# Rewriting the order of all steps in a fused GateLoop and SoLU kernel

## The chip, the cores and the metric

The kernel runs on one core of one Trainium2 chip. The metric is the device time of one execution in microseconds (us). A time quoted for a kernel is the median of its executions; stretches, waits and idle times are those of its one profiled execution. Every ratio is the mean time of one kernel's runs over the mean time of the other's runs of the same rounds, so it is not quite the ratio of the medians quoted beside it. An interval is a 95% interval of that ratio. All runs here were correct. Executions over 1.5% slower than the fastest of the same kernel are left out of the means.

In the lines of the profile, PE is TensorE, PEld its weight loads, DVE VectorE, ACT ScalarE, POOL GpSimd, and SP the engine that only issues transfers; a q marks an issuing queue. L1034 is a line of the kernel (the same line is L1032 after the change, whose text is two lines shorter). `A <- B: 17.1, 11, 2.7` says that A waited for B, for 17.1 us in all, 11 times, at most 2.7. A name such as `f_zT<-f_zd` gives what is written and what is read.

## The reference, cut to what matters

```python
def _attn_ref(q, k, v, a_re, a_im):          # (4, 8, 768, 48), float32
    mag = np.sqrt(a_re * a_re + a_im * a_im)
    scale = np.minimum(mag, 0.999) / (mag + 1e-06)
    a_re_n, a_im_n = (a_re * scale, a_im * scale)
    for t in range(S):                        # 768 steps of a complex-gated state
        ...
        y[:, :, t] = np.einsum('bhd,bhde->bhe', q[:, :, t], S_re)

def _moe_ref(x, w_in, w_out, g_ln):           # 3072 tokens, 384 -> 1024 -> 384
    h = x @ w_in
    ...                                       # sm = softmax of h over the 1024
    solu = h * sm
    ln = (solu - mu) / np.sqrt(var + 1e-06) * g_ln
    return (ln @ w_out).astype(np.float32)
```

## The kernel before: the parts that the change touches

The sequence is cut into 24 chunks of 128 tokens (six stretches of time for each of four batches). A chunk passes through these steps, each a small function with a name:

- `k2`, `q2` multiply k and q by their decays (VectorE). `kqb` turns the product in blocks of 32 (VectorE), and `kqt0`, `kqt1`, `kqt2` carry the blocks to their place with twelve transfers of 64 KB (in 22 of the 24 chunks; TensorE turns the other two). I call these **the turned blocks**. `score0`, `score1` multiply them (TensorE), `mask0` masks, `values` and `carry` finish the attention.
- `turn_x`, `turned_x`, `up0`, `up1` are the up projection. `exp0` and `solu0` make z. `blocks` turns z in blocks (VectorE), `away` writes them to DRAM with four transfers, `back` reads them with one, and `down0`, `down1` are the down projection (20 chunks; TensorE turns z in the other four).
- `load_*` fetch inputs for two chunks at once. `again` fetches a piece of the weights a second time, for a check that `inspect` makes.

```python
    KQ_ENGINES = nc.sync, nc.scalar, nc.scalar          # SP, ACT, ACT
...
        def blocked():                                   # step kqb
            t = st["kb"] = kbp.tile([P, 3, 2 * H, 32], FP, tag="kb", name="f_kb")
            nc.vector.transpose(out=t, in_=T["kq", c].rearrange("p n h (j f) -> p j (n h) f", f=32))

        def turned(i):                                   # steps kqt0, kqt1, kqt2
            ...
            for r in ((0, 1), (2,), (3,))[i]:            # six transfers by SP, then three and three by ACT
                for j in range(3):
                    eng = KQ_ENGINES[i]
                    eng.dma_start(out=T["kqT", c][j * 32:(j + 1) * 32, r], in_=st["kb"][r * 32:(r + 1) * 32, j])
...
        def away():
            st["zd"] = dram.tile([4, 32, 4, 32 * KF], FP, tag="zd", name="f_zd")
            for r in range(4):
                nc.sync.dma_start(out=st["zd"][:, :, r].rearrange("s f x -> f s x"),
                                  in_=st["zb"][r * 32:(r + 1) * 32].rearrange("p s t c -> p s (t c)"))

        def back():
            st["zT"] = zp.tile([P, P, KF], FP, tag="zT", name="f_zT")
            nc.sync.dma_start(out=st["zT"].rearrange("p t c -> p (t c)"),
                              in_=st["zd"].rearrange("s f r x -> (s f) (r x)"))
```

The order of everything is written by hand, as four strings of step names. The kernel schedules by hand, so each engine is given its instructions in the order in which the steps are written. In a loop of two chunks, `kqt0:2` means the step for chunk n + 2, and `square:g2` the step for the pair of chunks two ahead.

```python
    for s in START.split():
        ...
    for n in range(2, NC * B - 4):
        for s in (ODD if n % 2 else EVEN).split():
            nm, i = s.split(":")
            go(nm, n // GB + int(i[1:]) if i[0] == "g" else n + int(i))
    for s in END.split():
        ...
```

## Time and profile before

The median was 486.88 us in the first runs, and 487.02 us (483.74 to 488.56, four runs) in those that the result below is compared with.

| stretch, ended by TensorE's | length | TensorE idle | TensorE busy |
|---|---|---|---|
| end of the 6th up projection | 149.1 | 35.5 | 113.6 |
| end of the 20th (fourteen chunks of the loop) | 253.2 | 19.4 | 233.8 |
| last instruction | 75.5 | 4.1 | 71.4 |

Idle is the gap in front of TensorE's instructions, added up from the trace; busy is the rest. A last 6.8 us follow after TensorE, for 484.5 us in all. The lines of the page that carry this stand in the prediction below.

### The profile page before, as it was taken

What the parts mean: (1) busy time and instruction counts of PE and PEld (TensorE: products, weight loads), DVE (VectorE), ACT (ScalarE), POOL (GpSimd) and SP (SyncE); (2) the same over time, 40 slices, a digit from 0 to 9 for tenths busy, and PEclk for the clock granted to TensorE, in tenths of its full rate; (3) what the DMA queues carried; (4) which work ended last, traced back from release to release, by engine and by line L of the source; (5) the groups of instructions that cost most, each with busy time, mean ns of one, the idle gap of its engine ahead of it and who ended that gap; (6) DMA issues with size and microseconds to landing.
All of it is one profiled execution on the core that took longest, in us unless ns stands there. A gap on an engine that the chain in (4) does not pass through costs nothing.

```text
span 484.5 us, 14751 instructions
## 1 busy us (share of the span) xinstructions
PE 418.7 (86%) x6244; PEld 282.6 (58%) x6244; DVE 385.8 (80%) x555; ACT 266.6 (55%) x417; POOL 40.8 (8%) x110
## 2 busy tenths in 40 slices
PE   0257977999999988988989998998998997999994
PEld 0035544555676665566666676576675674577762
DVE  5889999798999889789789899689799788482430
ACT  4989967666654743753735654654753743522120
POOL 0000000000001101100110101101001001010010
PEclk9999987999999999999989999999999998999998
DMA  9887957948868769769669759659659758255321
GB/s 246 187 199 216 220 136 178 253 108 175 226 147 200 193 149 212 183 145 210 170 164 225 208 135 216 169 125 222 180 134 214 181 136 224 62 151 145 97 68 41
DMA packets 173419, 82.99 MB, mean 171 GB/s; under 512 B 145312, under 2 KB 158624, under 8 KB 173344
## 3 DMA queue, kind: packets, MB, share of 16 engines
q1 hardware_dynamic: 166864, 72.97, 62.8%
q10 hardware_dynamic: 6480, 8.99, 7.1%
q8 instruction: 51, 0.84, 0.8%
q14 instruction: 24, 0.20, 0.1%
HBM read 49.35 MB, written 15.20 MB: 133 GB/s over the span
## 4 chain that ended last, share of the span: by engine, by line
PE 38%; DMA 19%; DVE 17%; SPq 15%; issue 5%; ACT 4%; ACTq 0%; DVEq 0%
PE f_o L1064 17%; PE f_h L1003 9%; SPq L896 7%; DMA f_zT<-f_zd 6%; DMA f_kqT<-f_kb 5%; SPq L1034 4%; DMA f_zd<-f_zb 3%; DVE f_kb L888 3%; DVE f_kq L880 3%; DMA f_q<-in_q_dram 3%; PE f_score L937 2%; PE f_phase L830 2%; PE f_y L954 2%; DVE f_zb L1028 2%; SPq L648 2%
## 5 line engine op out<-in xcount | busy, mean ns | idle before, releaser
L1064 PE MATMUL f_o<-f_w_out,f_zT 128*128 128x384 f32 x384 | 140.9, 517 | 17.6 <-DMA f_zT<-f_zd 17.1
L1064 PEld LDWEIGHTS f_o<-f_w_out,f_zT 128*128 128x128 f32 x384 | 111.4, 298 | 38.3 <-ACT f_ar L783 12.9
L1003 PE MATMUL f_h<-f_w_in,f_xT 128*128 128x512 f32 x288 | 131.3, 600 | 0.6 <-issue 0.6
L1003 PEld LDWEIGHTS f_h<-f_w_in,f_xT 128*128 128x128 f32 x288 | 52.9, 190 | 56.6 <-issue 53.9
L1008 ACT ACTIVATE f_z<-f_h 128x1024 f32<-128x1024 f32 x24 | 24.5, 1023 | 54.8 <-PE f_h L1003 36.4
L888 DVE STREAM_TRANSPOSE f_kb<-f_kq 128x1536 f32<-128x1536 f32 x22 | 39.1, 1777 | 12.0 <-DMA f_kqT<-f_kb 11.6
L962 ACT COPY f_xn<-f_y 128x384 f32<-128x384 f32 x24 | 11.5, 478 | 64.1 <-PE f_y L957 48.3
L1011 DVE TENSOR_TENSOR f_z<-f_h,f_z 128x1024 f32<-128x1024 f32 x24 | 29.0, 1209 | 19.7 <-ACT f_z L1008 19.7
L1028 DVE STREAM_TRANSPOSE f_zb<-f_z 128x1024 f32<-128x1024 f32 x20 | 41.0, 2052 | 0.4
L937 PEld LDWEIGHTS f_score<-f_kqT 96*32 96x32 f32 x1536 | 29.9, 112 | 17.8 <-issue 16.6
L937 PE MATMUL f_score<-f_kqT 96*32 96x128 f32 (+3 forms) x1536 | 33.6, 239 | 6.6 <-issue 4.3
L776 PE MATMUL f_L<-f_lr,f_mats 128*128 128x384 f32 x48 | 20.4, 553 | 20.8 <-DVE f_lr L771 20.8
L941 DVE TENSOR_TENSOR f_att<-f_score,f_mats 128x1024 f32<-128x1024 f32 x24 | 29.1, 1211 | 6.8 <-PE f_score L937 6.7
L837 DVE SCALAR_TENSOR_TENSOR f_f<-f_f,f_phase 128x384 f32<-128x384 f32 x24 | 13.1, 549 | 26.0 <-ACT f_f L833 26.0
L957 PE MATMUL f_y<-f_state,f_kqT 96*32 96x48 f32 x1280 | 30.8, 206 | 0.0
L1052 DVE BATCH_NORM_STATS2 f_bs<-f_z 128x6 f32<-128x512 f32 x48 | 30.4, 671 | 0.0
L997 ACT COPY f_xT<-f_xt 128x384 f32<-128x384 f32 x24 | 11.4, 476 | 31.4 <-PE f_xt L993 22.6
L957 PEld LDWEIGHTS f_y<-f_state,f_kqT 96*32 96x32 f32 x1280 | 28.4, 110 | 0.2
L776 PEld LDWEIGHTS f_L<-f_lr,f_mats 128*128 128x128 f32 x48 | 9.9, 212 | 29.6 <-DVE f_lr L771 21.4
L954 PE MATMUL f_y<-f_v,f_att 128*32 128x48 f32 x768 | 25.6, 209 | 0.7 <-DVE f_att L941 0.7
L1057 POOL TENSOR_TENSOR f_s<-f_s,f_mv 128x1 f32<-128x1 f32 x24 | 5.0, 208 | 247.1 <-DVE f_mv L1053 247.1
L954 PEld LDWEIGHTS f_y<-f_v,f_att 128*32 128x32 f32 x768 | 16.4, 109 | 14.8 <-issue 11.1
(98 smaller groups left out, 662.1 us busy)
## 6 DMA issues: line engine op xcount, KB each, us to landing
f_zd<-f_zb SPq DMA_DIRECT2D x80, 128.0 KB, 2.7
f_zT<-f_zd SPq DMA_DIRECT2D x20, 512.0 KB, 3.9
f_kqT<-f_kb ACTq DMA_DIRECT2D x132, 64.0 KB, 3.7
f_kqT<-f_kb SPq DMA_DIRECT2D x132, 64.0 KB, 2.0
f_raw<-in_moe_w_out_dram SPq DMA_DIRECT2D x16, 384.0 KB, 4.2
f_raw<-in_moe_w_in_dram SPq DMA_DIRECT2D x12, 512.0 KB, 4.2
f_ar<-in_a_re_dram SPq DMA_DIRECT2D x12, 384.0 KB, 7.9
f_ai<-in_a_im_dram SPq DMA_DIRECT2D x12, 384.0 KB, 5.3
```

Of the source, the lines that this page charges most:

```text
L776: nc.tensor.matmul(out=ps, lhsT=tri, rhs=st["lr"][:, i * DM:(i + 1) * DM], start=True, stop=True)
L888: nc.vector.transpose(out=t, in_=T["kq", c].rearrange("p n h (j f) -> p j (n h) f", f=32))
L896: eng.dma_start(out=T["kqT", c][j * 32:(j + 1) * 32, r], in_=st["kb"][r * 32:(r + 1) * 32, j])
L937: nc.tensor.matmul(out=scores[r0:r0 + 32, x, r:], lhsT=QK[:, r // 32, x], rhs=QK[:, r // 32:, H + x], start=True, stop=True)
L941: nc.vector.tensor_tensor(out=st["att"].rearrange("p (i u) t -> p i u t", u=2), in0=scores.rearrange("p (i u) t -> p i u t", u=2), in1=mat ...
L954: nc.tensor.matmul(out=y[r:r + 32, hs], lhsT=st["att"][:, x, r:r + 32], rhs=rhs, start=True, stop=(ti == 0))
L957: nc.tensor.matmul(out=y[r:r + 32, hs], lhsT=T["kqT", c][:, r // 32, H + x], rhs=state[b][:, hs], start=False, stop=True)
L1003: nc.tensor.matmul(out=st["h"][:, half * 512:(half + 1) * 512], lhsT=st["xT"][:, c * P:(c + 1) * P], rhs=w_in[:, c, half * 512:(half + 1) ...
L1011: nc.vector.tensor_tensor(out=st["z"], in0=st["h"], in1=st["z"], op=OP.mult)
L1028: nc.vector.transpose(out=st["zb"].rearrange("p s t c -> p s c t"), in_=st["z"].rearrange("p (c s f) -> p s c f", s=4, f=32))
L1052: nc.vector.bn_stats(out=bs[:, i], in_=z[:, i * 512:(i + 1) * 512])
L1064: nc.tensor.matmul(out=st["o"], lhsT=st["zT"][:, c] if n in SHORT else st["zT"][:, :, c], rhs=w_out[:, c], start=(c == 0), stop=(c == KF - 1))
```

## The change

The intent was that short transfers (turned blocks, z) should no longer stand behind long loads in the DMA queues, and that k and q should be turned a chunk sooner. Only the four strings differ; no instruction was added or taken away. START and END are cut here, being lists of the same kind.

```diff
 EVEN = """
-again:1 values:0 phase0:g1 phase1:g1 qs1:g1 norm:-1 x:0 nearest0:g1 inspect:-1 carry:0 nearest1:g1 qs0:g1
-part0:g1 add:0 load_q:g2 turn_x:0 score1:1 last:g1 turned_x:0 again:8 scale:-2 part1:g1 score0:1 cos:g1 clamp:g2
-sin:g1 exp:g1 mask0:1 inverse:g2 up0:0 up1:0 back:-1 load_vr:g1 exp0:0 k2:2 q2:2 kqb:2 load_v:g2 values:1 kqt0:2
-ratio:g2 down0:-1 kqt2:2 solu0:0 zt0:0 x:1 turn_x:1 blocks:0 carry:1 down1:-1 kqt1:2 tangent:g2 turned_x:1
-away:0
+ratio:g2 blocks:0 kqt0:2 again:-5 tangent:g2 store:-2 turn_x:1 turned_x:1 qs1:g1 down1:-1 ends:g1 carry:1 norm:0
+scale:-1 square:g2 secant:g2 away:0 again:4 size:g2 turn_ends:g1 k2:3 kqt2:2 kqt1:2 up0:1 tot:g1 up1:1 score0:2
+score1:2 inspect:-2 add:1 eps:g2 lnm:g2 exp0:1 back:0 store:-1 total1:g2 q2:3 fourth:g2 mask0:2 total0:g2 kqb:3
+grow1:g2 down0:0 decay1:g2 decay0:g2 grow0:g2 trig:g2 solu0:1
 """
 ODD = """
-square:g2 secant:g2 fourth:g2 ks1:g1 ends:g1 up0:0 load_k:g2 k2:2 q2:2 back:-1 score0:1 zT0:-1 score1:1
-load_ai:g3 zt1:-1 turn_ends:g1 size:g2 load_ar:g3 scale:-2 eps:g2 kqb:2 add:0 lnm:g2 tot:g1 mask0:1 zT1:-1 up1:0
-kqt0:2 norm:-1 kqt2:2 exp0:0 total1:g2 grow1:g2 inspect:1 total0:g2 grow0:g2 store:-2 decay1:g2 solu0:0 ks0:g2
-decay0:g2 store:-3 trig:g2 angle:g2 kqt1:2 blocks:0 on:g2 down0:-1 away:0 down1:-1
+down1:-1 load_ai:g3 load_ar:g3 qs0:g2 angle:g2 kqt0:2 on:g2 blocks:0 ks1:g2 kqt1:2 kqt2:2 inspect:-6 phase0:g2
+load_vr:g2 values:1 away:0 phase1:g2 nearest0:g2 x:1 score1:2 nearest1:g2 part0:g2 turn_x:1 clamp:g3 score0:2
+turned_x:1 carry:1 part1:g2 cos:g2 load_v:g2 up0:1 up1:1 ks0:g2 back:0 sin:g2 mask0:2 exp:g2 inverse:g3 add:1
+last:g2 values:2 load_k:g3 load_q:g3 k2:3 scale:-1 exp0:1 q2:3 down0:0 norm:0 x:2 kqb:3 solu0:1
 """
```

More of the change, by code (lines that the diff above doesn't have):

```diff
@@ L515 @@
 START = """
-load_ar:0 load_ai:0 clamp:0 fetch:8 fetch:2 fetch:0 fetch:1 inverse:0 ratio:0 raised:8 raised:2 tangent:0
-square:0 secant:0 convert:2 size:0 fourth:0 eps:0 fetch:5 convert:8 raised:0 load_k:0 raised:1 lnm:0 total0:0
-load_q:0 load_ai:1 convert:1 grow0:0 decay0:0 total1:0 ks0:0 decay1:0 grow1:0 convert:0 trig:0 angle:0 qs0:0
-load_ar:1 last:0 fetch:13 raised:5 fetch:3 phase0:0 ks1:0 nearest0:0 convert:5 phase1:0 nearest1:0 part0:0
-part1:0 ends:0 load_q:1 cos:0 sin:0 turn_ends:0 exp:0 fetch:4 clamp:1 k2:0 load_v:0 qs1:0 tot:0 kt0:0 q2:0
@@ L521 @@
-inverse:1 kT0:0 qt0:0 kt1:0 qT0:0 k2:1 raised:3 qt1:0 ratio:1 kT1:0 load_vr:0 qT1:0 raised:13 kt0:1 fetch:10
-tangent:1 square:1 q2:1 score0:0 kT0:1 score1:0 qt0:1 secant:1 raised:4 convert:3 mask0:0 values:0 size:1
-convert:13 qT0:1 x:0 fetch:6 fetch:7 fourth:1 turn_x:0 turned_x:0 kt1:1 fetch:9 raised:6 convert:4 kT1:1
-raised:9 load_ai:2 eps:1 carry:0 convert:6 fetch:12 raised:10 convert:9 load_vr:1 fetch:11 raised:7 qt1:1 up0:0
-add:0 up1:0 lnm:1 qT1:1 convert:10 total0:1 total1:1 carry:1 exp0:0 gain:0 mean:0 decay0:1 score1:1 convert:7
@@ L526 @@
-load_k:1 grow0:1 solu0:0 add:1 decay1:1 qs0:1 grow1:1 score0:1 load_ar:2 trig:1 mean:1 angle:1 raised:12 ks0:1
-phase0:1 load_k:2 last:1 phase1:1 ks1:1 mean:2 qs1:1 mask0:1 convert:12 nearest0:1 nearest1:1 raised:11 part0:1
-part1:1 again:0 values:1 clamp:2 cos:1 mean:3 load_vr:3 ends:1 again:1 sin:1 x:1 exp:1 turn_x:1 mean:4
-convert:11 again:4 inverse:2 zt0:0 k2:2 mean:5 q2:2 kqb:2 turned_x:1 zT0:0 load_ai:3 kqt0:2 kqt1:2 k2:3 kqt2:2
-mean:6 ratio:2 mean:7 tangent:2 q2:3 square:2 secant:2 turn_ends:1 zt1:0 centre:0 fourth:2 centre:7 load_q:2
@@ L531 @@
-up0:1 centre:5 centre:4 up1:1 zT1:0 score0:2 size:2 eps:2 again:2 kqb:3 exp0:1 load_ar:3 tot:1 kqt0:3 centre:1
-score1:2 kqt1:3 load_v:1 lnm:2 centre:3 total1:2 centre:6 total0:2 decay1:2 centre:2 norm:0 solu0:1 down0:0
-grow0:2 inspect:2 again:6 grow1:2 decay0:2 inspect:0 again:8 zt0:1 trig:2 angle:2 zt1:1 zT0:1 kqt2:3 down1:0
-mask0:2 on:2 load_v:2 load_v:3 zT1:1 ks0:2
+load_ar:0 load_ai:0 clamp:0 fetch:1 fetch:8 inverse:0 ratio:0 tangent:0 raised:1 raised:8 square:0 fetch:5
+convert:1 secant:0 fourth:0 size:0 eps:0 lnm:0 raised:5 fetch:6 raised:6 total1:0 convert:8 total0:0 grow1:0
@@ new lines @@
+load_k:0 decay1:0 load_ar:1 convert:6 fetch:2 load_q:0 grow0:0 decay0:0 ks1:0 trig:0 ks0:0 gain:0 last:0 angle:0
+phase0:0 convert:5 load_ai:1 raised:2 fetch:0 phase1:0 convert:2 nearest0:0 nearest1:0 part0:0 fetch:3 part1:0
+cos:0 sin:0 exp:0 mean:0 ends:0 fetch:4 clamp:1 qs0:0 k2:0 q2:0 inverse:1 kt0:0 k2:1 qt0:0 qs1:0 kT0:0 qT0:0
+load_vr:0 kt1:0 kT1:0 ratio:1 qt1:0 qT1:0 q2:1 load_v:0 turn_ends:0 tangent:1 score0:0 score1:0 kt0:1 raised:4
+fetch:11 fetch:7 raised:0 tot:0 mask0:0 qt0:1 kT0:1 raised:3 values:0 x:0 convert:4 qT0:1 raised:11 turn_x:0
@@ new lines @@
+turned_x:0 convert:0 qt1:1 square:1 carry:1 load_ai:2 kt1:1 up0:0 convert:3 raised:7 fetch:9 secant:1 add:1
+fourth:1 fetch:10 carry:0 fetch:13 convert:11 size:1 up1:0 kT1:1 raised:9 load_q:1 eps:1 convert:7 load_vr:1
+mean:1 raised:10 add:0 convert:9 mean:2 qT1:1 lnm:1 total0:1 load_k:1 raised:13 exp0:0 grow0:1 total1:1 score0:1
+score1:1 convert:10 fetch:12 convert:13 mean:3 decay1:1 mean:4 solu0:0 mask0:1 decay0:1 grow1:1 trig:1 angle:1
+qs0:1 ks1:1 values:1 phase1:1 ks0:1 phase0:1 mean:5 qs1:1 raised:12 convert:12 nearest1:1 load_ar:2 mean:6
@@ new lines @@
+mean:7 nearest0:1 part1:1 part0:1 cos:1 load_k:2 sin:1 x:1 load_v:1 exp:1 load_v:2 turn_x:1 last:1 zt0:0 clamp:2
+centre:3 turned_x:1 centre:6 k2:2 q2:2 inverse:2 zt1:0 kqb:2 centre:7 kqt0:2 ratio:2 up0:1 zT1:0 kqt2:2 kqt1:2
+centre:2 zT0:0 tangent:2 centre:1 square:2 load_ai:3 up1:1 score0:2 score1:2 centre:4 secant:2 load_ar:3
+centre:5 centre:0 fourth:2 size:2 down0:0 k2:3 mask0:2 eps:2 exp0:1 lnm:2 load_q:2 ends:1 turn_ends:1 values:2
+tot:1 total1:2 q2:3 x:2 solu0:1 decay1:2 kqb:3 grow1:2 total0:2 load_vr:2 decay0:2 grow0:2 down1:0 trig:2
@@ L535 @@
+angle:2 zt0:1 ks0:2 turn_x:2 ks1:2 carry:2 kqt0:3 zT0:1 turned_x:2 zt1:1 zT1:1 on:2 add:2 phase1:2 phase0:2
+kqt1:3 nearest1:2 kqt2:3 up0:2 nearest0:2 norm:0 scale:0 clamp:3 part1:2 part0:2 again:2 score0:3 load_q:3
+score1:3 cos:2 up1:2 load_vr:4 sin:2 norm:1 exp:2 down0:1 inspect:2 qs0:2 exp0:2 inverse:3 again:0 k2:4 mask0:3
+q2:4 solu0:2 again:4 values:3 zt0:2 zt1:2 x:3 kqb:4 last:2 carry:3 load_k:3 again:6 zT0:2 zT1:2
 """
 EVEN = """
-again:1 values:0 phase0:g1 phase1:g1 qs1:g1 norm:-1 x:0 nearest0:g1 inspect:-1 carry:0 nearest1:g1 qs0:g1
@@ L548 @@
 """
 END = """
-ks1:11 phase0:11 nearest0:11 values:20 norm:19 back:19 phase1:11 x:20 part0:11 turn_x:20 nearest1:11 score1:21
-turned_x:20 part1:11 score0:21 mask0:21 qs0:11 cos:11 load_vr:11 sin:11 up0:20 exp:11 k2:22 scale:18 q2:22
-up1:20 down0:19 kqb:22 exp0:20 kqt0:22 solu0:20 blocks:20 values:21 kqt2:22 kqt1:22 x:21 down1:19 norm:20
-turn_x:21 scale:19 qs1:11 k2:23 score0:22 turned_x:21 score1:22 q2:23 away:20 back:20 up0:21 kqb:23 up1:21
-mask0:22 values:22 down0:20 kqt0:23 kqt1:23 down1:20 store:19 exp0:21 last:11 x:22 kqt2:23 store:18 turn_x:22
@@ L555 @@
-turned_x:22 scale:20 solu0:21 score0:23 score1:23 blocks:21 mask0:23 away:21 back:21 up0:22 up1:22 values:23
-store:20 down0:21 norm:21 exp0:22 solu0:22 x:23 turn_x:23 blocks:22 turned_x:23 down1:21 ends:11 scale:21
-away:22 up0:23 up1:23 back:22 down0:22 down1:22 exp0:23 store:21 solu0:23 norm:22 zt0:23 scale:22 zT0:23 zt1:23
-down0:23 norm:23 zT1:23 down1:23 store:22 scale:23 store:23
+k2:23 turn_x:21 kqt0:22 down1:19 turned_x:21 store:18 norm:20 kqt2:22 up0:21 kqt1:22 score1:22 blocks:20 qs1:11
@@ new lines @@
+score0:22 away:20 back:20 q2:23 kqb:23 scale:19 up1:21 mask0:22 ends:11 kqt0:23 kqt2:23 kqt1:23 values:22
+down0:20 exp0:21 x:22 down1:20 turn_x:22 score0:23 score1:23 turned_x:22 solu0:21 up0:22 blocks:21 away:21
+back:21 mask0:23 scale:20 store:20 values:23 x:23 up1:22 exp0:22 turn_x:23 solu0:22 blocks:22 turned_x:23
+down0:21 store:19 away:22 norm:21 up0:23 norm:22 back:22 up1:23 down1:21 exp0:23 solu0:23 scale:21 zt0:23
+store:21 zT0:23 down0:22 down1:22 zt1:23 norm:23 scale:22 down0:23 zT1:23 store:22 down1:23 scale:23 store:23
```

## The prediction

> **What bounds the kernel now.** I read first the busy times of the page, then a table of four stretches of the span, then TensorE's waits, and last the waits and the timeline of the queue SP, which issues nearly all transfers.
>
> The page's first part, busy time of each engine:
>
> ```profile
> PE 418.7 (86%) x6244; PEld 282.6 (58%) x6244; DVE 385.8 (80%) x555; ACT 266.6 (55%) x417; POOL 40.8 (8%) x110
> ```
>
> The same by stretch. Columns: stretch and length, busy time of PE, weight load, DVE, ACT, POOL, then the granted clock, the DMA share and GB/s:
>
> ```profile
> 0.00:40.00 40.00, 13.10 (x87) 7.77 (x91) 29.29 (x56) 30.55 (x45) 0.68 (x5) 1.00 0.85 220
> 40.00:100.00 60.00, 51.42 (x664) 29.95 (x656) 54.98 (x90) 45.66 (x73) 3.14 (x10) 0.91 0.81 191
> 100.00:440.00 340.00, 316.87 (x5168) 217.63 (x5169) 287.08 (x383) 182.82 (x285) 33.40 (x83) 0.99 0.73 174
> 440.00:484.50 44.50, 37.30 (x355) 27.25 (x341) 14.49 (x28) 7.58 (x16) 3.54 (x12) 0.96 0.28 83
> ```
>
> TensorE is the bound: busy 93% of the long middle (316.87 of 340). All its idle time is 484.5 - 418.7 = 65.8 us: 26.9 in the first 40 us, 8.6 up to 100, 23.1 in the middle, 7.2 at the end. VectorE is close behind (287.08 of 340, 84%), and the 16 DMA engines are 73% busy there. No order can win more than the idle time, and a good part of it is unavoidable latency at both ends. What ended TensorE's waits (total, times, longest):
>
> ```profile
> PE f_L L776 <- DVE f_lr L771: 20.8, 2, 18.6
> PE f_o L1064 <- DMA f_zT<-f_zd: 17.1, 11, 2.7
> PE f_turned L902 <- DVE f_kq L880: 4.5, 2, 4.2
> PE f_score L937 <- issue: 4.3, 6, 1.1
> PE f_score L937 <- DMA f_kqT<-f_kb: 2.3, 3, 1.0
> ```
>
> 18.6 us of it is the start, before any data is there. In the middle the line that matters is the second: eleven times the down projection waited some 1.5 us for z, which is turned through DRAM (VectorE blocks, four transfers away, one back). How that transfer is late stands in SP's timeline (start, duration, issued transfer):
>
> ```profile
> 283.17 0.39 SPq L648 DMA_DIRECT2D f_v<-in_v_dram  x1
> 283.67 4.49 SPq L896 DMA_DIRECT2D f_kqT<-f_kb  x6
> 288.25 2.16 SPq L1034 DMA_DIRECT2D f_zd<-f_zb  x4
> 290.46 0.43 SPq L648 DMA_DIRECT2D f_k<-in_k_dram  x1
> 293.82 0.34 SPq L1039 DMA_DIRECT2D f_zT<-f_zd  x1
> ```
>
> VectorE's timeline has z's block transpose at 282.42 for 2.07 us, so z was ready at 284.5. The transfer away was issued at 288.25, because SP stood in the six issues of the turned k and q. Back was issued at 293.82 and the down projection began at 297.54 after a wait of 1.93. So 13.0 us passed from ready to used, of which 3.8 only stood in line. The four transfers away also share the engines with the loads of v and k.
>
> **What the Trainium skill says.** (1) "DMA: Bandwidth & Descriptors", section "Issuing engines are not separate DMA queues": transfers from all issuers run on the same 16 engines and interleave. The trace agrees as far as it shows: turned blocks issued on ACT land after 3.7 us (median), those issued on SP after 2.0, so a second issuer does not escape the traffic. (2) Same page, "Specifications": below 512 B a transfer isn't at line rate. Here 145312 of 173419 packets are that small; the loads of 384 KB are 2048 packets of 192 B, and take 5.2 to 7.9 us from issue to landing against 3.9 for the 512 KB of z coming back. A load ahead in the queue is dear. (3) "TensorE: Matmul & The Clock Gate", part 1: after an idle time the array's clock halves for some us. Agrees: four phase matmuls took 2.93 us right after an idle of 3.12, and 1.49 when warm; the granted clock was 0.91 in the stretch 40 to 100. (4) "Perfetto Trace Analysis", "Optimization Strategy": look for the gaps of the engine to be optimised and what ends them, which is the way taken above.
>
> **The change part by part.** No instruction is added or removed and no tile or buffer count changes; only the order in which steps are written, and with it the order on every engine. So the 418.7 us of TensorE work and the DMA bytes stay, and everything is about waits.
>
> *The loop's transfers.* Before, the six SP transfers of turned k and q stood between the loads and z's transfers, in both halves of the two-chunk loop. In the new even half they come first (the blocks were made at the end of the half before), then z away, then z back, and all five long loads are in the odd half. (Only the weight pieces fetched a second time, for a check, still ride in the even half, beside z, in most pairs.) For an even chunk I expect ready to used: 2.2 us of issue + 2.7 landing + 3.9 to 4.5 back = 9 to 9.5 us, not 13.0: some 3.5 us sooner, more than the wait of 1.9 there. For an odd chunk the load of v and four small loads still stand near z's two transfers, so I expect little. The distance in TensorE work between up and down projection, added up from the rows, hardly changes for an even chunk (about 16.2 us in both). Of the 17.1 us I take away 9 to 11.
>
> *k and q a chunk sooner.* Doubling, blocks and transfers of chunk n+1 come before the odd up projection's results are consumed, and the scores of n+1 are made earlier. The score waits (4.3 + 2.3 us) may shrink. Yet in the odd half the ACT half of the turned blocks is issued after four exponentials, a table load and the arctangent, near the time when the score wants it; my hand schedule has it some 1.5 us late. Net: 0, from +2 to -5.
>
> *VectorE.* By the same rows it has 31.6 us of work for two chunks (86% of a period of 36.4, which is (406.26 - 151.41)/7 between down projections). TensorE without gaps would need 36.4 - 2.8 = 33.6. So once TensorE's waits shrink, VectorE is at 94% and must come in the right order; in the new order its waits for the rounding step on ACT (26.0 us before) have a load of other work between, but blocks, masks and z products each wait on TensorE. I charge 3 us in all for new waits of this kind.
>
> *Clock.* The dips after waits cost 60 x 0.09 = 5.4 us in the stretch 40 to 100, and about 1.8 us each twice later. With fewer long gaps I take back half, 4 us.
>
> *Start and end.* The first wait of 18.6 is a chain load, invert, logarithm, exponent; the new order has the same transfers and ACT steps ahead of it (two weight pieces, in the other order), so within 0.5 us the same. Between 40 and 100 us TensorE idles 8.6; the new order weaves the weight conversion differently and I take 3. At the end, the last chunk's exponent and product are now written before the down projection of the chunk before, not after: 1 us.
>
> Sum: 10 + 0 - 3 + 4 + 3 + 1 = 15 us. 486.9 - 15 = 472.
>
> **Rivals.** (a) *VectorE becomes the bound.* For it: 84% busy in the middle, 31.6 against 33.6 a period. It would hold the period near 35.5; gain 7 us or less, 480. Against it: its own waits in the middle (22.9 for the rounding step, 11.6 for the block buffer) are of the kind that an order removes. (b) *The wait moves from z to the scores.* All long loads are now in one half; if they pile up in front of the turned blocks or the odd chunk's z, TensorE waits there as long as it did for z. For it: DMA share 0.83 to 0.88 in every other 20 us already. Result 482 to 488, about the same. (c) *The order was found well everywhere* and nearly all the middle's idle goes: 23 + 4 + 5 of clock, 455 to 460. Against it: three resources over 80% leave little room for a hitch.
>
> **Range and chances.** The centre is 472. Rivals (a) and (b) pull up, (c) down; the range 459 to 484 holds 8 in 10. Faster by over 2% means under 477.1: 0.66. Within 2%: 0.28, mostly (a) and (b). Slower than 496.6 would need a new repeated wait of over 1 us a chunk: 0.06.
>
> **What would show it.** Right: down projection waits on z fall from 17.1 to about 7 us; z's ready-to-used time for even chunks near 9 us; the period between down projections falls from 36.4 to near 35; TensorE busy time as such falls by a few us through the clock (418.7 to about 414); the idle of the first 40 us unchanged at 26 to 28. Wrong: score waits on turned blocks rise above 10 us (rival b), or VectorE busy in the middle above 92% with TensorE waiting for it (rival a). If the middle is unchanged and the gain lies in the first 100 us, I was right for the wrong reason.

## More of the kernel before

I call blocks, away and back **z's way out and back**.

One line is added here, from the busy times of one stretch (its columns as in the prediction: stretch, length, busy PE, weight load, DVE, ACT, POOL, clock, DMA share, GB/s). It is the steady part that later kernels are held against:

```profile
150.00:400.00 250.00, 230.64 (x3850) 161.96 (x3849) 214.99 (x291) 139.34 (x217) 25.63 (x62) 0.99 0.76 178
```

TensorE is busy for 230.64 of 250 us (92%) and VectorE for 214.99 (86%). Anything that wins must fill TensorE's gaps. Two more lines, from the waits of SP's queue, become important only later. The first is the time for which z's way out (L1034) stood in SP for turned blocks of ACT:

```profile
SPq L1034 <- DMA f_kqT<-f_kb: 1.3, 1, 1.3
SPq L896 <- DMA f_kqT<-f_kb: 25.2, 12, 7.1
```

That is one wait of 1.3 us in the whole run. The second line is the same kind of wait at SP's own block issues, which stand ahead of z: 25.2 us.

## The result and the profile after

The changed kernel took 512.5 us (509.38 to 515.64, four runs) against 487.02. The ratio is 1.0533 (1.0445 to 1.062): it is **slower by 5.3%**. All outputs are right.

The page's busy times after:

```profile
PE 427.4 (83%) x6244; PEld 285.7 (56%) x6244; DVE 387.6 (76%) x555; ACT 265.2 (52%) x417; POOL 48.9 (10%) x110
```

The span grew by 27.4 us (484.5 to 511.9). TensorE was busy 8.7 us longer for the same 6244 instructions, and idle for the other 18.7. The four stretches after, with the same columns as in the prediction:

```profile
0.00:40.00 40.00, 15.46 (x163) 9.60 (x163) 29.96 (x58) 30.84 (x45) 0.45 (x5) 0.83 0.87 220
40.00:100.00 60.00, 48.64 (x579) 27.89 (x580) 51.94 (x85) 43.60 (x71) 4.10 (x9) 0.91 0.69 155
100.00:440.00 340.00, 300.60 (x4668) 204.53 (x4670) 273.32 (x365) 173.49 (x272) 38.85 (x78) 0.96 0.69 168
440.00:511.90 71.90, 62.66 (x855) 43.66 (x842) 32.40 (x49) 17.22 (x31) 5.47 (x18) 0.98 0.39 107
```

In the long middle TensorE, VectorE and the DMA engines are all less busy than before, and the granted clock is lower. No resource became the bound: something stands in line. Cut at the same events as before, the time went here:

| stretch | length | TensorE idle | TensorE busy |
|---|---|---|---|
| to the 6th up projection | 153.9 (+4.8) | 40.2 (+4.7) | 113.7 (+0.1) |
| to the 20th | 272.6 (+19.4) | 32.0 (+12.6) | 240.6 (+6.8) |
| to the last instruction | 78.6 (+3.1) | 5.4 (+1.3) | 73.2 (+1.8) |

So the loss is mainly a loss of the loop: 19.4 us in fourteen chunks. What ended TensorE's waits after:

```profile
PE f_L L774 <- DMA f_raw<-in_moe_w_in_dram: 17.8, 1, 17.8
PE f_score L935 <- DMA f_kqT<-f_kb: 16.0, 8, 4.3
PE f_o L1062 <- DMA f_zT<-f_zd: 13.6, 8, 2.9
PE f_score L935 <- issue: 8.6, 7, 3.1
PE f_score L935 <- DMA f_vr<-in_v_dram: 5.1, 1, 5.1
```

The waits for z have hardly shrunk (17.1 to 13.6). The scores, which had waited for 6.6 us, now wait for turned blocks and others for 29.7 us by these lines. The clock follows. The trace has eleven stretches of half clock after and five before, most 3.4 us long. One down projection right after a wait took 7.22 us, against 5.52 for one in the trace before.

How the blocks and z came late is seen in one even half. SP's timeline after (start, duration, what is issued):

```profile
257.70 5.38 SPq L894 DMA_DIRECT2D f_kqT<-f_kb  x6
263.13 0.58 SPq L677 DMA_DIRECT2D f_raw<-in_moe_w_in_dram  x1
...
264.31 5.76 SPq L1032 DMA_DIRECT2D f_zd<-f_zb  x4
272.48 0.34 SPq L1037 DMA_DIRECT2D f_zT<-f_zd  x1
```

ACT's timeline in the same microseconds (the bracket is the idle time ahead and what ended it):

```profile
263.13 0.58 ACT L1067 ACTIVATE f_ot<-f_o,f_rs 128x384 f32<-128x384 f32 x1 [2.29 <-PE f_o L1062]
...
264.54 5.09 ACTq L894 DMA_DIRECT2D f_kqT<-f_kb  x6
269.68 0.93 ACT L765 ACTIVATE f_u<-f_lr,f_bias 128x768 f32<-128x768 f32 x1 [4.27 <-DMA f_kqT<-f_kb]
```

The blocks were ready at 256.74. SP issued its six from 257.70, after a load of q. ACT issued its six only from 264.54, since `kqt2:2 kqt1:2` are written behind `scale:-1` (the line at 263.13), which waits for the down projection of the chunk before. The scores began at 271.92, after 2.58 us of waiting for them.

z's blocks were ready at 261.66. SP's way out began at 264.31, but its four issues took 5.76 us, although an issue that waits for nothing takes 0.4 to 0.6. SP's waits in z's way out give the reason:

```profile
SPq L1032 <- DMA f_kqT<-f_kb: 13.6, 8, 4.3
SPq L1032 <- DMA f_raw<-in_moe_w_in_dram: 8.9, 3, 3.3
SPq L1032 <- DMA f_raw<-in_moe_w_out_dram: 6.5, 3, 2.4
```

z's way out waits 29.0 us in all for transfers with which it shares no data: ACT's turned blocks and the repeated fetch of weights. In the traces of both kernels the transfers of SP and ACT together signal eight semaphores (counters on which instructions wait), and by the waits in the built program a transfer isn't issued before the last one on its semaphore has landed. This is the build's choice, not the change's. It was there before too, and SP waited for it then as well: 25.2 us at its own block issues, but only 1.3 at z's way out. The new order puts ACT's blocks and the repeated fetch beside z's way out, and the waits fall on z's four issues.

### The profile page after: what moved, and what is told of

Same layout as the page of the kernel before. It is cut to its first block, busy times and chain, and to the rows that moved or that the text cites. A ratio compares the mean times of both kernels' runs of the same rounds, so it can differ in the third digit from the quotient of the medians.

```text
span 511.9 us, 14742 instructions
## 1 busy us (share of the span) xinstructions
PE 427.4 (83%) x6244; PEld 285.7 (56%) x6244; DVE 387.6 (76%) x555; ACT 265.2 (52%) x417; POOL 48.9 (10%) x110
## 4 chain that ended last, share of the span: by engine, by line
PE 50%; DMA 20%; ACT 7%; SPq 7%; DVE 6%; issue 5%; ACTq 2%; POOL 0%; DVEq 0%; POOLq 0%
PE f_o L1062 18%; PE f_h L1001 13%; DMA f_kqT<-f_kb 11%; PE f_score L935 6%; SPq L894 4%; DMA f_zT<-f_zd 3%; DMA f_zd<-f_zb 3%; PE f_L L774 3%; PE f_y L952 2%; ACTq L894 2%; PE f_phase L828 2%; PE f_y L955 2%; PE f_d L968 2%; SPq L646 2%; PE f_xt L991 2%
## 5 line engine op out<-in xcount | busy, mean ns | idle before, releaser
L1062 PE MATMUL f_o<-f_w_out,f_zT 128*128 128x384 f32 x384 | 140.6, 516 | 14.6 <-DMA f_zT<-f_zd 13.6
L1001 PE MATMUL f_h<-f_w_in,f_xT 128*128 128x512 f32 x288 | 133.6, 612 | 0.0
L1001 PEld LDWEIGHTS f_h<-f_w_in,f_xT 128*128 128x128 f32 x288 | 54.1, 195 | 59.1 <-issue 57.3
L935 PE MATMUL f_score<-f_kqT 96*32 96x96 f32 (+3 forms) x1536 | 38.9, 253 | 32.1 <-DMA f_kqT<-f_kb 16.0
L935 PEld LDWEIGHTS f_score<-f_kqT 96*32 96x32 f32 x1536 | 33.9, 119 | 49.8 <-issue 40.9
L1009 DVE TENSOR_TENSOR f_z<-f_h,f_z 128x1024 f32<-128x1024 f32 x24 | 28.8, 1200 | 17.1 <-ACT f_z L1006 17.0
L831 ACT ACTIVATE f_f<-f_phase,f_bias 128x384 f32<-128x384 f32 x24 | 13.9, 580 | 51.2 <-PE f_phase L828 39.7
L1055 POOL TENSOR_TENSOR f_s<-f_s,f_mv 128x1 f32<-128x1 f32 x24 | 9.5, 394 | 306.1 <-DVE f_mv L1051 306.1
L774 PE MATMUL f_L<-f_lr,f_mats 128*128 128x384 f32 x48 | 22.4, 598 | 18.5 <-DMA f_raw<-in_moe_w_in_dram 17.8
L1067 ACT ACTIVATE f_ot<-f_o,f_rs 128x384 f32<-128x384 f32 x24 | 13.8, 575 | 36.5 <-PE f_o L1062 22.1
L765 ACT ACTIVATE f_u<-f_lr,f_bias 128x768 f32<-128x768 f32 x12 | 11.2, 934 | 30.2 <-DMA f_kqT<-f_kb 26.8
L952 PE MATMUL f_y<-f_v,f_att 128*32 128x48 f32 x768 | 25.5, 209 | 1.1 <-DVE f_att L939 1.1
```

Source lines behind the costliest of these rows:

```text
L774: nc.tensor.matmul(out=ps, lhsT=tri, rhs=st["lr"][:, i * DM:(i + 1) * DM], start=True, stop=True)
L935: nc.tensor.matmul(out=scores[r0:r0 + 32, x, r:], lhsT=QK[:, r // 32, x], rhs=QK[:, r // 32:, H + x], start=True, stop=True)
L952: nc.tensor.matmul(out=y[r:r + 32, hs], lhsT=st["att"][:, x, r:r + 32], rhs=rhs, start=True, stop=(ti == 0))
L1001: nc.tensor.matmul(out=st["h"][:, half * 512:(half + 1) * 512], lhsT=st["xT"][:, c * P:(c + 1) * P], rhs=w_in[:, c, half * 512:(half + 1) ...
L1009: nc.vector.tensor_tensor(out=st["z"], in0=st["h"], in1=st["z"], op=OP.mult)
L1062: nc.tensor.matmul(out=st["o"], lhsT=st["zT"][:, c] if n in SHORT else st["zT"][:, :, c], rhs=w_out[:, c], start=(c == 0), stop=(c == KF - 1))
```

## The experiments

Two theories were put first. **Q**: the even chunk's ACT blocks are written too late. **Z**: the repeated fetch and its semaphores hold z. A third suspect was the five long loads, now all in the odd half. In the tables "loop" is the stretch from the 6th to the 20th up projection, as above; times from a chunk's blocks or z being ready are means over chunks 6 to 19.

**1. Turned blocks early.** EVEN alone is edited:

```diff
-ratio:g2 blocks:0 kqt0:2 again:-5 ... size:g2 turn_ends:g1 k2:3 kqt2:2 kqt1:2 up0:1 ...
+ratio:g2 blocks:0 kqt0:2 kqt2:2 kqt1:2 again:-5 ... size:g2 turn_ends:g1 k2:3 up0:1 ...
```

> Changed kernel with one edit: in the even half the six transfers of turned k and q that ACT issues are written at the front of the half, not after the square and the logarithm. Theory A (late issue): in the changed kernel they go out only after the scale of the chunk before, square and logarithm, at about 7 us into the half; they hold up the score (1.3 to 2.6 us a pair of chunks), the exponentials of eps behind them, and the last two pieces of z going away, whose DMA semaphore they held. Then score waits on turned blocks fall from 16 to under 9 us, ready-to-used of z for even chunks from about 14 to 13, and the time from 512.5 to about 500 (498 to 506). Rival B (the DMA engines as a whole are the limit) : the blocks land as late as before because loads of q and k stand ahead of them; time within 1% of 512. Rival C (VectorE's new order is the limit): also within 1%.

It took 510.76 us, ratio 1.0462 (1.0381 to 1.0543). TensorE's waits between 150 and 430 us:

```profile
PE f_o L1062 <- DMA f_zT<-f_zd: 28.7, 8, 4.7
PE f_score L935 <- issue: 1.6, 2, 0.8
```

The score waits of the loop went from 18.0 to 1.6 us. In the even half, the one edited, they went from 9.5 to 0.0, and ACT's last block issue from 11.2 us after the blocks were ready to 3.9: theory Q names the cause of these. The odd half's went from 8.5 to 1.6, though SP's blocks went out later there (from 5.3 us after ready, not 2.6); TensorE now waited for z first, so this is no proof for that half, to which experiment 3 belongs. The waits for z rose from 13.6 to 25.4 in the loop, which still takes 270.4 us, and the time missed theory A's 498 to 506. The first stretch recovered (149.9 against 153.9).

**2. The repeated fetch late.** EVEN alone again:

```diff
-... kqt0:2 again:-5 tangent:g2 ... away:0 again:4 size:g2 ... back:0 store:-1 ...
+... kqt0:2 tangent:g2 ... away:0 size:g2 ... back:0 again:-5 again:4 store:-1 ...
```

> Changed kernel with one edit: in the even half the two repeated weight fetches are written after z's way back, not ahead of and inside z's way out. Theory A: one of the four pieces of z waited until the fetch of 384 to 512 KB had landed, and the turned blocks on ACT shared the engines with it; without it z's ready-to-used time for even chunks falls by about 2 us of 14, time to about 500 (497 to 507). Rival B: total DMA traffic counts and not its order: within 1% of 512.

It took 511.36 us, ratio 1.0463 (1.0398 to 1.0529). TensorE's waits in the same window:

```profile
PE f_score L935 <- DMA f_kqT<-f_kb: 20.6, 8, 5.1
PE f_o L1062 <- DMA f_zT<-f_zd: 2.8, 2, 2.2
```

The mirror image: z's waits fell from 13.6 to 3.5 in the loop, and the score waits rose from 18.0 to 31.0. In even chunks z's way back was issued 6.8 us after z was ready and not 9.5, so Z names a cause of z's waits; how much of their fall came from the scores' longer waits, which give z time, was not separated. The loop took 274.5, and the time missed theory A's 497 to 507.

**3. Long loads behind the blocks.** In ODD, `load_ai` and `load_ar` were moved:

```diff
-down1:-1 load_ai:g3 load_ar:g3 qs0:g2 ... kqt1:2 kqt2:2 inspect:-6 ... turn_x:1 clamp:g3 score0:2 ... inverse:g3 ...
+down1:-1 qs0:g2 ... kqt1:2 kqt2:2 load_ai:g3 load_ar:g3 inspect:-6 ... turn_x:1 score0:2 ... clamp:g3 inverse:g3 ...
```

> Changed kernel with one edit: in the odd half the loads of a are written after the turned blocks and not ahead of them (the clamp that reads them follows later, so that VectorE does not wait). Theory A: the first SP piece of the turned blocks was issued only when the load of a's imaginary part had landed (2.4 us late), which made the odd half's score wait 1 to 3 us; that wait goes, z's way out of the odd half starts 1 to 2 us sooner; time to about 504 (500 to 510), as even-half waits stay. Rival B or C: within 1% of 512.

It took 516.89 us, ratio 1.057 (1.0501 to 1.0639). The wait ahead of the odd half's scores vanished (1.0 us a pair to 0.0) but that ahead of the even half's grew (1.4 to 2.1), and the loop took 277.1. With the waits between a chunk's score matmuls counted too, the odd half's went from 8.5 to 3.0 us in the loop and the even half's from 9.5 to 14.4. So the loads of a ahead of the blocks were a cause of the odd half's waits, but the gain in time that the theory expected did not come.

**4. All three edits.**

> All three edits together. Theory A: the period of two chunks falls from 38.9 us to 35 to 36, time 480 to 490, about the kernel before or a little below it. Rival B: 505 to 512, with waits on z or on turned blocks as large as before at other places. Rival C: TensorE's waits move to VectorE's masks and products, period 37.5 or more, time 500 or more.

It took 528.52 us, ratio 1.0823 (1.0759 to 1.0887). My expectation of a gain missed by far: the waits for z were 27.2 us in the loop.

**5. The edits of 1 and 2 together**, since 3 might have spoilt the sum.

> Changed kernel with the first two edits together (ACT's turned blocks to the front of the even half; repeated weight fetches after z's way back). Theory D (two dependent chains of nearly the same length, one through the turned blocks and the scores, one through z; each edit shortens one and the other then sets the period): the score waits stay under 3 us in the loop as with the first edit, and the z waits fall from 25 to about 14 us, time 496 to 503. Rival E (the issue queue SP and the eight DMA semaphores are the limit, so that each edit only shifts who waits): 505 to 513, waits on z still over 20 us.

It took 526.83 us, ratio 1.0703 (1.0567 to 1.0839); the loop 287.2, with 25.5 us of waits for z and 12.2 for scores. Two edits that each remove one wait do worse together than either alone, and the time missed both theories. So what is written early may be delaying something in SP's order. That order in experiment 1:

```profile
250.75 0.38 SPq L646 DMA_DIRECT2D f_k<-in_k_dram  x1
256.55 0.38 SPq L646 DMA_DIRECT2D f_q<-in_q_dram  x1
257.04 4.43 SPq L894 DMA_DIRECT2D f_kqT<-f_kb  x6
262.69 2.07 SPq L1032 DMA_DIRECT2D f_zd<-f_zb  x4
```

SP waits between the loads of k and q (there 58.6 us over the whole run for ACT's blocks), then issues six blocks, and only then z's way out.

**6. A middle place.** The edit of 2, with `kqt2:2 kqt1:2` after `turned_x:1`.

> As the run before, but ACT's turned blocks stand in the middle of the even half, after the copy of turned x and ahead of scale and square, so that SP's loads of q and its own six blocks don't wait on their semaphores. Theory D: blocks issued 3 to 4 us sooner than in the changed kernel, without the late start of SP's blocks that the front position brought; even-half z used within 12 us of the block transpose, not 14; time 488 to 498. Rival E: 505 or more.

It took 507.22 us, ratio 1.0362 (1.0245 to 1.0479): the best of these, and still slower than before. z's waits were 3.7 us and the score waits 24.5 in the loop. Where the blocks are written moves the wait; it doesn't remove it.

**7 to 9. Take SP's six blocks out of SP.** This is one line, put into the changed kernel (7), into the kernel before (8), and into the kernel of experiment 1 (9):

```diff
-    KQ_ENGINES = nc.sync, nc.scalar, nc.scalar
+    KQ_ENGINES = nc.gpsimd, nc.scalar, nc.scalar
```

> Changed kernel with the six SP transfers of turned blocks a chunk issued by GpSimd instead, with semaphores of their own. If SP's order and its semaphores hold z up (rival E), z's way out starts at once and the time falls to 495 or less. If ACT's late issue of the other half of the blocks is what counts (theory D), score waits stay at 15 us or more and the time stays within 1.5% of 512.

> Kernel before with the same edit: SP's turned blocks issued by GpSimd. In the kernel before z's way out waits 4 to 5 us behind these six issues in both halves; if that is what makes the down projection wait (14.4 us in the loop), those waits go and the time falls by 2 to 3%, 472 to 480. If GpSimd's slower issue or its own waits delay the blocks, scores wait instead: 487 or more.

> Changed kernel, SP's six turned blocks issued by GpSimd (its z waits fell to zero but its scores waited 25.6 us in the loop for ACT's six blocks) and those ACT blocks at the front of the even half. Theory D, both chains relieved at once: score waits in the loop under 5 us, z waits under 5 us, time 470 to 485. If something else in the new order holds the loop (rival C, VectorE's order): over 495 with TensorE waiting on VectorE or ACT.

| order | blocks of SP stay | blocks of SP go to GpSimd |
|---|---|---|
| before | 1 | 462.83 us, 0.9468 (0.939 to 0.9546) |
| changed | 512.5 us, 1.0533 | 514.8 us, 1.0536 (1.0438 to 1.0633) |
| changed, ACT's blocks early (1) | 510.76 us, 1.0462 | 471.8 us, 0.9645 (0.9582 to 0.9709) |

The ratios are each against the kernel before in the same rounds; the cells were measured in different rounds. The transfers that GpSimd issues signal eight other semaphores, so the edit takes SP's blocks out of SP's order and off the shared semaphores at once.

In the changed order neither edit moves the time by more than 1%, which is within the noise of the intervals, and both together turn +5.3% into -3.5%. TensorE's waits between 150 and 430 us for number 7:

```profile
PE f_score L935 <- DMA f_kqT<-f_kb: 12.4, 5, 3.9
PE f_score L935 <- DMA f_ai<-in_a_im_dram: 8.1, 2, 4.4
```

and the steady stretch for number 9:

```profile
150.00:400.00 250.00, 241.83 (x4037) 170.98 (x4040) 230.62 (x308) 146.63 (x229) 75.26 (x154) 1.00 0.81 198
```

With SP relieved alone, z's waits are 0 but ACT's late blocks hold the scores (25.6 us in the loop, 23.4 of it in the even half, where experiment 9 has 0.0). With both, the loop takes 239.2 us with 8.2 idle, TensorE at 97% and VectorE at 92%. **So the changed order loses by two coupled delays: ACT's blocks written late, and six block issues of SP that stand in front of z.** Undoing one hands the wait to the other. The second delay is not new, though: the same line gains 5.3% in the old order too. With SP relieved in both orders the changed one is 11.2% slower than the old (514.8 against 462.83 us), and with ACT's blocks early as well 1.9% (471.8, in other rounds). So what the change itself made worse is, in the main, the place of ACT's blocks.

Number 8 is the fastest kernel, faster than both and than its expectation of 472 to 480: the old order with one line changed. Its loop takes 232.7 us with 2.9 idle. SP's waits there:

```profile
SPq L1034 <- DVE f_zb L1028: 76.1, 17, 10.4
SPq L1034 <- DMA f_kqT<-f_kb: 6.9, 8, 2.4
```

z's way out now mostly waits for z itself: SP is there first. Before, it was issued 4.7 and 4.1 us after z was ready (even and odd chunks); now 0.0 and 0.4. SP's waits for turned blocks and other loads are still there (6.9 us at z's way out, and as much for reversed v; 22.6 at the loads of inputs) and TensorE hardly waits. So such waits, where they stand in that order, do little harm.

**10. The middle place with GpSimd**: the change of 9, with `kqt2:2 kqt1:2` after `turned_x:1`.

> The same with ACT's blocks in the middle of the even half (after the copy of turned x). Theory D: nearly the same as at the front, 468 to 485, a little better if at the front the loads of q still wait for the semaphores of ACT's blocks. Rival C: over 495.

It took 479.92 us, ratio 0.9816 (0.9771 to 0.9861): between 7 and 9.

**11 and 12. All twelve blocks to GpSimd**, in the changed order and in the old.

> Changed kernel with its written order untouched: all twelve transfers of turned blocks of a chunk issued by GpSimd, none by SP or ACT. Theory D: ACT's exponentials (eps) no longer stand behind six issues, and blocks no longer behind scale, square and logarithm; but GpSimd's own order puts them behind the small operations of the layer norm. 470 to 490. Rival C: over 495.

> Kernel before with all twelve issued by GpSimd. With six of twelve moved its loop was already 98.8% busy on TensorE, so little is left: 458 to 468; if twelve issues of 0.5 us make the blocks late (6 us), scores wait and it is 470 or more.

They took 571.08 us, ratio 1.1626 (1.1548 to 1.1704), and 479.15, ratio 0.9786 (0.972 to 0.9852). The first was a clear miss; the second fell in the worse branch of its expectation, with 5.4 us of score waits in the loop. GpSimd has an order too. Its waits in number 11:

```profile
POOL f_s L1055 <- DVE f_mv L1051: 160.4, 20, 19.7
```

The blocks stand there behind the small layer-norm operations of `norm`, which wait for VectorE: in the even half the last of the twelve goes out 13 to 16 us after the blocks are ready. Scores waited for 59.7 us in the loop. The place in the issuer's order is what counts here, on GpSimd as on SP.

**13 and 14. Loads of k and q to GpSimd, blocks left with SP**, in the order of experiment 1 and in the changed order. This asks whether SP was held by the loads' waits for semaphores (58.6 us in experiment 1) or by its own six blocks. (`load` is also given the issuing engine as an argument.)

```diff
-            load_k=load("k", k, ldv) ... load_q=load("q", q, ldv)
+            load_k=load("k", k, ldv, nc.gpsimd) ... load_q=load("q", q, ldv, nc.gpsimd)
```

> Edit: the order of e1 (the turned blocks of an even chunk all written early), and the two loads of k and q issued by GpSimd in place of SP; the turned blocks stay with SP and ACT. In e1 SP stood 58.6 us before its loads of k and q for transfers of ACT's turned blocks, and z went down late (28.7 us of waits). Theory, the semaphores: it was this wait of the loads that held SP's order; with the loads gone from SP its six blocks start at once, z goes down on time, f_o waits in the loop fall below 10 us, and the time is 485 to 498 us, ratio 0.99 to 1.02. Rival, SP's own time of issue: the six blocks stand before the way out of z whenever they are issued there; f_o waits stay above 18 us and the time is above 500 us, ratio above 1.025.

> Edit: the changed kernel with the two loads of k and q issued by GpSimd alone. The control of e12. Theory, the semaphores: in the changed kernel the turned blocks of even chunks are late since ACT issues them late, which this leaves; score waits in the loop stay at 15 to 20 us and the time within 1.5% of the changed kernel, 505 to 520 us. Rival: the loads themselves held SP in the changed kernel too; then the time falls below 500 us with the order left as it is.

They took 526.42 us, ratio 1.0746 (1.0653 to 1.0839), and 530.23, ratio 1.0864 (1.0773 to 1.0956). In the first, the waits for z stayed (28.9 us in the loop, all in even chunks):

```profile
PE f_o L1062 <- DMA f_zT<-f_zd: 28.9, 7, 5.4
```

By these numbers the rival of that expectation came true, but not quite its reason. With the loads off SP, z's way out began sooner in even chunks (2.6 us after z was ready, 4.6 in experiment 1) and so did the way back (8.0 and 10.0); yet from there to the use of z took 6.2 us and not 4.0, so nothing was won. Why the way back took longer was not tested. The control missed both expectations: score waits of 25.2 us in the loop, and a first stretch of 163.4 us against 153.9. Part of that stretch is the first wait, now 21.6 us for f_L. SP's timeline in number 13:

```profile
286.24 6.53 SPq L894 DMA_DIRECT2D f_kqT<-f_kb  x6
292.82 2.09 SPq L656 DMA_DIRECT2D f_vr<-in_v_dram  x4
295.01 2.51 SPq L1032 DMA_DIRECT2D f_zd<-f_zb  x4
```

This is an odd chunk, for whose z TensorE did not wait, but it shows the six blocks at work. z's blocks were ready at 286.67 and left at 295.01, after six blocks that took 6.53 us to issue and four small loads. Six blocks a chunk earlier in the same trace took 3.79. So part of the 6.53 is SP's own issue time and part is waits. **The two were not separated**: I found no way to give the transfers more semaphores without changing who issues them.

## Why the prediction was wrong, point by point

It said 472 us; the result was 512.5. The sum of its terms beside what the traces show (idle by what it stood in front of, in us gained):

| term | predicted | measured |
|---|---|---|
| waits for z | +10 | +2.9 (17.5 to 14.6) |
| waits of scores | 0 (+2 to -5) | -25.6 (6.6 to 32.2) |
| clock | +4 | -8.7 (TensorE's busy time) |
| VectorE, start, end | +1 | +4.1 (all other idle), and -0.1 behind TensorE |
| sum | +15 | -27.4 |

**The scores are the step that failed.** The prediction said "Net: 0, from +2 to -5", with the odd half's ACT blocks "some 1.5 us late". It looked for ACT's late issue in the wrong half: in the odd half ACT's last issue came 3.5 us after the blocks (5.6 before), in the even half, behind `scale:-1`, 11.2 (4.1 before). And it read "a chunk sooner" as slack. But the scores are written sooner too: from blocks ready to scores begun took 11.6 and 15.8 us before (even and odd, mean of the loop), and 13.9 and 10.5 after. The two chunks together have 3.0 us less, while the last of an even chunk's twelve issues comes 11.2 us after the blocks (by ACT) and not 8.8 (by SP). Experiments 1 and 9 show the written place to be the cause of the even half's waits (9.5 us of the loop's 18.0); for the odd half's 8.5, experiment 3 points to the loads of a ahead of SP's blocks.

**z's way out failed as well.** "For an even chunk I expect ready to used ... 9 to 9.5 us" counted 2.2 us for the four issues. They take 5.5 us on average in the even half, and ready to used is 13.7 (before, as a mean, 14.0): z's way out does begin sooner (1.6 us after ready, 4.7 before), and its own issues lose the gain. I had seen SP "in the six issues" ahead of z, and took them as the only thing that could stand there. I never asked what a transfer waits for apart from its data. The prediction even noted that the weight pieces "still ride in the even half, beside z"; in experiment 2, without them there, the four issues took 3.8 us and the waits for z fell to 3.5 us in the loop.

**The clock** was expected to follow the gaps, and it did: the sign was that of the gaps, which was wrong. One reading of it was loose: the matmuls of 2.93 us, given beside a granted clock of 0.91, ran in the first 40 us, where the record of the clock shows 1.00.

**Rival (b)** had the right place, the scores, and its test was met ("score waits on turned blocks rise above 10 us": 16.0). Its reason, long loads piled up in front of the blocks, held for part of the odd half's waits (8.5 to 3.0 us in experiment 3), but moving two of these loads away won no time. It also expected no worse than 488 us. **Rival (a)** fell: VectorE was less busy, and with VectorE at 92% in the loop of number 9 TensorE still reached 97%. **The start** was nearly right: 17.8 against 18.6 us for the first wait. The 3 us expected between 40 and 100 us didn't come: TensorE's idle time there rose from 8.6 to 11.4. The chance of slower, 0.06, rested on "a new repeated wait of over 1 us a chunk"; that is what came: 18.0 us of score waits in fourteen chunks, 3.8 before.

What stays open: the share of the shared semaphores against SP's own issue time, and why taking the wait from one chain lengthens the other so much that the loop hardly changes (272.6 us, then 270.4 and 274.5 in experiments 1 and 2). I would explain it so, without having shown it. The turned blocks and z each form a ring of steps through the same in-order queues, both near 39 us for two chunks. The period between down projections was 36.4 us before and 39.1 after.

## What to carry to other kernels

Reordering steps changes the order of every in-order issuer, so for each transfer ask what stands ahead of it there, and also which unrelated transfers it must see land first. When undoing a suspect moves a wait to another place without moving the time, look for a second chain on the same queue and relieve both at once: neither edit alone gained over 1% here (within the noise), and both gained 8.4% of the changed kernel's time (ratio 1.0533 to 0.9645, each against the kernel before in its own rounds). Before rewriting an order, try taking the transfers that stand in the way out of that queue; one line did more here than the whole rewritten order.

## What the Trainium skill lacked or had wrong

- "DMA: Bandwidth & Descriptors", section "Issuing engines are not separate DMA queues": it says that initiating transfers on several engines "will only save the time on the sequencer it takes to initiate the DMA, which is usually small relative to the DMA itself". Moving six issues from SP to GpSimd gave 0.9468. The blocks themselves became slower (4.3 us median from issue to landing, against 2.0 on SP). What was won is seen in SP's order: z's way out was issued 4.7 us after it was ready before, and 0.0 after, in even chunks (the blocks also left the shared semaphores; the two were not separated). The section doesn't tell of what stands behind an issue in its queue.
- No page that I read tells that transfers of two issuers may be given the same few completion semaphores when a program is built, so that one transfer waits for another with which it shares no data. The changed kernel's z waited 29.0 us in this way, and SP's loads 58.6 us in experiment 1.
- "TensorE: Matmul & The Clock Gate", part 1: nothing wrong was found. Its windows of about 3.4 us agree with the trace (most stretches of half clock last 3.4 us).
